# One expert moved out of the last token group, its neighbour's sums rewritten around their swap, and the last drain in 128x64 tiles

## The chip, the cores and the metric

One core of a Trainium2 chip. The metric is the device time of one execution in microseconds (us); the time before is the median of three runs.

## The reference

Two blocks in a row. The first is an attention with a polynomial sketch (batch 4, 4 heads, 1088 positions, head size 32) whose output is laid out as 4352 tokens of 128 features. The second is a mixture of 8 experts over all tokens, weighted by a Sinkhorn-normalised routing. The change is in the second block alone:

```python
def _moe_ref(x, w_gate, w1, w2):
    N, D = x.shape                      # 4352, 128
    E = w_gate.shape[1]                 # 8
    logits = x @ w_gate
    ...                                 # P: 8 Sinkhorn rounds over exp(logits)
    out = np.zeros((N, D), dtype=np.float32)
    for e in range(E):
        h = np.maximum(x @ w1[e], 0.0)  # hidden size 1024
        ye = h @ w2[e]
        out += P[:, e:e + 1] * ye
    return out.astype(np.float32)
```

All of it is in fp32. Inside the profile one fp32 matmul of the program shows as two matmul records and two weight loads.

## The kernel before, in words

The attention, the routing and some experts for the first tokens run first; the change does not touch them. The function `weighted()` does the rest, in the token groups of the list `wgroups`: a group is a start, a width `n` and a list of experts, and holds 2n tokens in two halves. Five groups of 2 x 256 tokens go through experts 1 to 7, three of 2 x 224 through experts 2 to 7, one of 2 x 224 (tokens 3904 to 4351) through experts 2, 1, 3, 4, 5, and the last group takes the same tokens through the experts left. The order of experts is turned round in every other group, so that neighbours share a loaded expert. Each group adds its result to what `kept` holds for its tokens.

Both layers are cut into 2 x 2 blocks. A product of blocks in 64x64 tiles is one unit of TensorE's work: four matmuls (two row halves, two column halves), eight records. The first layer takes seven products instead of eight for each half of an expert, by sums of inputs, of weights and of results. So does the second layer, except in groups listed in `whole` (the last group), which take eight products and need fewer sums: four sums of hidden activations on VectorE (L1099 to L1104) fall away there.

The work is a list of steps `todo`: one for each group's expert and each half `s` of it. In the loop at the end of `weighted()` the generators `firsts(t)` (first layer of step t) and `seconds(t - 1)` (second layer of the step before) take turns, product by product. So a step interleaves 7 products of the first layer (L1043, into the PSUM tiles `pair`) with 7 or 8 of the second (L1193, into the PSUM tiles `s`, called `acc`). In `firsts` ScalarE copies three results out (L1122 to L1132), VectorE adds three pairs of them (L1053), ScalarE applies the ReLU (L1056). The next step's first product writes over the `pair` tile that the third add reads. The last `seconds` runs alone, since no first layer is left.

`acc[g][rho][u]` are four PSUM banks of a group: `rho` is the row half that a 64-row matmul used, `u` the token half (in the seven-product form, q). The two banks of one `u` have to be added in the end.

At the end of a group of seven products `ended()` copies two banks out with ScalarE (tile `z`), `add_half()` adds the other two with VectorE (L1242), and `finish_seven()` swaps the upper and lower 64 partitions of `z` into `w` by two DMAs on SP (L1260). The sums after that are put into the list `leisure`. An entry is taken from it by `leave()` at fixed places of later steps, some by GpSimd, most by VectorE; an entry `None` only lets one such place pass. `put()` turns a token half with VectorE (`yt`, L1278), and `store()` writes it out with 4 or 8 DMAs (L681), four for each batch row that it touches. `finish_last()` is the end of the last group: it does what is left in `leisure`, adds both banks to `kept`, turns and stores.

The order is the program's own on each engine and each DMA queue (`tc.manual_schedule()`), so whatever waits holds back what stands behind it. SP issues the DMAs of loads, swaps and stores in one line; only the stores of the last group are shared with ScalarE's queue.

Of the kernel before, what the change touches and what calls it, by code (L numbers as in the profile page):

```python
# [10 lines left out]
F32 = mybir.dt.float32  # L11
# [39 lines left out]
def kernel(  # L51
# [477 lines left out]
    def routing():  # L529
# [45 lines left out]
        for b in (1, 0, 2, 3):  # L575
# [99 lines left out]
    def store(yt, b0, b1, queues=(nc.sync,)):  # L675
        first, k = b0, 0
        while b0 < b1:
            b, a = divmod(b0, SA)
            m = min(b1 - b0, SA - a)
            for r in range(4):  # L680
                queues[k % len(queues)].dma_start(  # L681
                    out=AP(tensor=out.tensor, offset=out[b * S + a, 32 * r].offset,
                           ap=[[SA * DM, 32], [DM, m], [1, 32]]),
                    in_=yt[32 * r:32 * (r + 1), b0 - first:b0 - first + m, :])
                k += 1
            b0 += m
# [323 lines left out]
    def weighted():  # L1010
# [8 lines left out]
        def flat(t, n):  # L1019
            return t.rearrange("p (r n) -> p r n", r=2)  # L1020
# [6 lines left out]
        def firsts(t):  # L1027
# [137 lines left out]
        def seconds(t):  # L1165

            i, s = todo[t]
            g, e = witems[i]
            lo, n, es = wgroups[g]
            h, ts = rooms(t)  # L1170
            coming = next_of(i, 2) if s else None

            def fetch(part_):
                if coming is not None:
                    load_second(coming, part_)

            if g not in acc:
                acc[g] = [[mps.tile([P, 512], F32, tag=f"s{2 * rho + q}", name="s") for q in range(2)]
                          for rho in range(2)]

            def raw(dh, k, r):
                m = ((RAW00, RAW01), (F0, RAW11))[dh][k]
                return form_of(i, m)[:, H2 * (2 * r + s):H2 * (2 * r + s + 1)]

            def form(m, r):
                return form_of(i, (F0, F1, F2, F3)[m])[:, H2 * (2 * r + s):H2 * (2 * r + s + 1)]

            def into(half, w, x, r, q, place):
                per = 2 * len(es) * (3 if q and g != LAST else 4)
                for rho in range(2):  # L1190
                    rows = slice(H2 * rho, H2 * (rho + 1))
                    c = counts[g, rho, q, half] = counts.get((g, rho, q, half), 0) + 1
                    yield lambda rho=rho, rows=rows, c=c: nc.tensor.matmul(  # L1193
                        acc[g][rho][q][H2 * half:H2 * (half + 1), n * place:n * (place + 1)], w[rows],
                        flat(x, n)[rows, r], start=c == 1, stop=c == per, tile_position=(H2 * rho, H2 * half))

            def both(x, y):
                for one, two_ in zip(x, y):
                    one()
                    two_()  # L1200

            last = t + 1 == len(todo) or witems[todo[t + 1][0]][0] != g
            if g in whole:
                for m, (k, u, b) in enumerate(((0, 0, 0), (1, 0, 2), (0, 1, 3), (1, 1, 1))):
                    for r in range(2):
                        both(into(0, raw(0, k, r), h[:, b], r, u, u), into(1, raw(1, k, r), h[:, b], r, u, u))
                        if last and m % 2 and r == 1:
                            finish_last(g, u)
# [22 lines left out]
        ends = {}  # L1231

        def ended(g, q):
            n = wgroups[g][1]
# [4 lines left out]
        def add_half(g, q):  # L1239
            n = wgroups[g][1]  # L1240
            z = ends[g][:, q, 0:2 * n]
            nc.vector.tensor_tensor(z, acc[g][1][q][:, 0:2 * n], z, op=Alu.add)  # L1242

        def settle(g):
            while chores and chores[0][0] <= g:
# [6 lines left out]
        def finish_seven(g):  # L1252
# [5 lines left out]
            t = late[0].tile([P, 3, NW], F32, tag="t", name="t", bufs=1)  # L1258
            for s in range(2):
                nc.sync.dma_start(out=w[H2 * (1 - s):H2 * (2 - s), :, 0:2 * n], in_=z[H2 * s:H2 * (s + 1), :, 0:2 * n])  # L1260
            leisure.extend([None] * (5 if g + 1 == LAST else 3))
# [11 lines left out]
            plus(y[up, 0], t1[up], t3[up])  # L1273
            out_of(g, y)

        def put(y, at, n, queues=(nc.sync,)):
            yt = late[0].tile([P, NW // 32, 32], F32, tag="yt", name="yt", bufs=2)[:, 0:n // 32, :]
            nc.vector.transpose(out=yt.rearrange("p b d -> p (b d)"), in_=y)  # L1278
            store(yt, at // 32, (at + n) // 32, queues)

        def out_of(g, y):
            lo, n, es = wgroups[g]
            for t in range(2):
                at = lo + n * (1 - t)
                k = kept[0][:, at:at + n]
                plus(k if g + 1 == LAST else y[:, t], y[:, t], k)
                if g + 1 < LAST:
                    leisure.append((lambda engine, t=t, at=at: put(y[:, t], at, n), False))

        def finish_last(g, u):  # L1290
            lo, n, es = wgroups[g]
            while leisure:
                do = leisure.pop(0)
                if do:
                    do[0](nc.vector)
            at = lo + n * (1 - u)
            y = kept[0][:, at:at + n]
            for rho in range(2):
                nc.vector.tensor_tensor(y, acc[g][rho][u][:, n * u:n * (u + 1)], y, op=Alu.add)
            put(y, at, n, (nc.sync, nc.scalar))  # L1300

        for t in range(len(todo) + 1):
            if t < len(todo):
# [145 lines left out]
```

## Time and profile before

| | |
|---|---|
| median of 3 runs | 894.93 us (894.17 to 895.25) |
| profiled execution | 893.78 us |
| its span | 892.0 us |
| PE, share of the span | 884.2 us, 99% |
| DVE | 758.1 us, 85% |
| ACT | 546.3 us, 61% |
| POOL | 271.0 us, 30% |
| granted TensorE clock | 1.0 |

PE is TensorE, PEld its weight loads, DVE VectorE, ACT ScalarE, POOL GpSimd, SP the queue of DMA issues. Rows of a timeline give start and duration in us, engine, line, operation, written and read tiles, shapes, count, and in brackets the idle time before with what ended it. The chain of waits is the work that ended last, followed back. Line numbers are those of the kernel before.

### The profile page before, as it was taken

To read this page: it belongs to the slowest core of one execution; us is meant where nothing else is said; L and a number is where in the kernel's file an instruction comes from. 1 tells how busy PE (TensorE), PEld (TensorE's weight loads), DVE (VectorE), ACT (ScalarE), POOL (GpSimd) and SP (SyncE) were. 2 spreads that over 40 slices of the span, in tenths; PEclk is the share of its full clock that TensorE was granted. 3 is DMA by queue.
4 is the path that set the end of the run, shared out by engine and by line. 5 is a ranking of instruction groups with operands and counts; after the bars stand their busy time and mean duration, and the time that the engine had idled before them with its cause. 6 is when DMAs were issued, how large, how long until landed. Compare 5 with 4: busy or idle time off the path is not lost.

```text
span 892.0 us, 36526 instructions
## 1 busy us (share of the span) xinstructions
PE 884.2 (99%) x15372; PEld 630.1 (71%) x15372; DVE 758.1 (85%) x1324; ACT 546.3 (61%) x1087; POOL 271.0 (30%) x307
## 2 busy tenths in 40 slices
PE   9999999999999999999999999999999999999997
PEld 5777644557666777777777777777877887887876
DVE  7578789887998888888888888888898899889885
ACT  3446366645666666666666666666666666666664
POOL 3121126364552223223213312322333222323220
PEclk9999999999999999999999999999999999999999
DMA  9998499686785876487567666665775875885752
GB/s 247 294 282 251 104 237 252 107 231 184 237 259 166 238 218 194 125 233 211 171 170 206 204 174 194 206 174 160 231 221 142 255 212 152 232 256 147 230 172 44
DMA packets 146628, 178.83 MB, mean 200 GB/s; under 512 B 56448, under 2 KB 93904, under 8 KB 146080
## 3 DMA queue, kind: packets, MB, share of 16 engines
q1 hardware_dynamic: 138832, 166.40, 64.5%
q0 software_dynamic: 6528, 9.95, 5.6%
q8 instruction: 122, 2.00, 0.9%
q14 instruction: 42, 0.34, 0.1%
q10 hardware_dynamic: 1104, 0.15, 0.1%
HBM read 133.83 MB, written 25.99 MB: 179 GB/s over the span
## 4 chain that ended last, share of the span: by engine, by line
PE 96%; DVE 2%; ACT 1%; issue 0%; POOL 0%; DVEq 0%; ACTq 0%; POOLq 0%
PE pair L1043 39%; PE s L1193 39%; PE a L711 7%; PE s L772 7%; PE a L305 1%; DVE hb L726 1%; PE a L420 1%; PE a L118 1%; PE a L272 0%; PE s L334 0%; PE a L384 0%; PE s L350 0%; DVE cs L560 0%; PE a L454 0%; PE a L350 0%
## 5 line engine op out<-in xcount | busy, mean ns | idle before, releaser
L1043 PE MATMUL pair<-xf,w1x 64*64 64x256 f32 (+1 forms) x6736 | 496.4, 365 | 0.1
L1043 PEld LDWEIGHTS pair<-xf,w1x 64*64 64x64 f32 x6736 | 255.4, 133 | 93.7 <-DVE hb L1053 6.1
L1053 DVE TENSOR_TENSOR hb<-pair,copies 128x512 f32<-128x512 f32 (+1 forms) x354 | 233.7, 662 | 69.3 <-PE pair L1043 29.9
L1193 PE MATMUL s<-hb,w 64*64 64x256 f32 (+1 forms) x3904 | 290.0, 364 | 0.0
L1193 PE MATMUL s<-hb,ws 64*64 64x256 f32 (+1 forms) x2848 | 213.6, 365 | 0.0
L1056 ACT ACTIVATE hb<-hb 128x512 f32<-128x512 f32 (+1 forms) x240 | 145.6, 608 | 102.0 <-DVE hb L1053 96.7
L1193 PEld LDWEIGHTS s<-hb,w 64*64 64x64 f32 x3904 | 151.9, 133 | 50.2
L973 POOL TENSOR_TENSOR xf<-xT,pb 128x512 f32<-128x512 f32 (+1 forms) x60 | 73.7, 1228 | 263.2 <-ACT xf L1066 216.2
L981 POOL TENSOR_TENSOR xf<-xf 128x512 f32<-128x512 f32 (+1 forms) x59 | 72.5, 1229 | 217.4 <-ACT xf L1066 133.3
L1193 PEld LDWEIGHTS s<-hb,ws 64*64 64x64 f32 x2848 | 111.4, 133 | 36.0
L711 PE MATMUL a<-xT,w 128*64 128x416 f32 (+3 forms) x512 | 121.1, 466 | 0.0
L713 ACT ACTIVATE hb<-a 128x416 f32<-128x416 f32 (+3 forms) x128 | 59.7, 468 | 66.1 <-PE a L711 53.5
L1056 ACT ACTIVATE hb<-pair 128x512 f32<-128x512 f32 (+1 forms) x126 | 72.5, 575 | 43.5 <-PE pair L1043 43.5
L1099 DVE SCALAR_TENSOR_TENSOR hb<-hb 128x512 f32<-128x512 f32 (+1 forms) x116 | 77.9, 671 | 16.5 <-ACT hb L1056 4.6
L1132 ACT COPY copies<-pair 128x512 f32<-128x512 f32 (+1 forms) x118 | 66.5, 564 | 30.6 <-PE pair L1043 30.6
L1129 ACT COPY copies<-pair 128x512 f32<-128x512 f32 (+1 forms) x118 | 66.5, 564 | 29.7 <-PE pair L1043 29.7
L1122 ACT COPY copies<-pair 128x512 f32<-128x512 f32 (+1 forms) x118 | 66.6, 565 | 26.4 <-PE pair L1043 26.4
L1102 DVE TENSOR_TENSOR hb<-hb 128x512 f32<-128x512 f32 (+1 forms) x116 | 77.8, 670 | 3.1 <-ACT z L1237 0.5
L1104 DVE TENSOR_TENSOR hb<-hb 128x512 f32<-128x512 f32 (+1 forms) x116 | 78.9, 680 | 0.0
L1103 DVE SCALAR_TENSOR_TENSOR hb<-hb 128x512 f32<-128x512 f32 (+1 forms) x116 | 78.8, 679 | 0.0
L726 DVE TENSOR_TENSOR hb<-hb 128x416 f32<-128x416 f32 (+7 forms) x84 | 60.5, 720 | 18.4 <-ACT hb L713 12.9
L772 PE MATMUL s<-hb,ws 128*64 128x416 f32 (+3 forms) x224 | 70.9, 475 | 0.6 <-DVE hb L726 0.4
(177 smaller groups left out, 668.2 us busy)
## 6 DMA issues: line engine op xcount, KB each, us to landing
w1x<-w1x SPq DMA_DIRECT2D x135, 256.0 KB, 4.0
w<-w2x SPq DMA_DIRECT2D x102, 256.0 KB, 4.0
ws<-w2x SPq DMA_DIRECT2D x50, 256.0 KB, 3.1
pb<-pT SPq DMA_DIRECT2D x35, 256.0 KB, 4.1
xf<-xf SPq DMA_DIRECT2D x70, 128.0 KB, 2.5
ws<-w2x SPq DMA_DIRECT2D x52, 128.0 KB, 3.6
w1x<-w1x SPq DMA_DIRECT2D x7, 896.0 KB, 5.0
w1x<-w1x SPq DMA_DIRECT2D x45, 128.0 KB, 3.8
```

Source lines behind the costliest of these rows:

```text
L711: nc.tensor.matmul(ph[sl], loaded_w[j][0][:, P * f + H2 * s:P * f + H2 * (s + 1)], xT[:, at + lo:at + hi], start=True, stop=True, tile_pos ...
L772: nc.tensor.matmul(sums[g][i][H2 * s:H2 * (s + 1)], w, x, start=c == 1, stop=c == per, tile_position=(0, H2 * s))
L973: nc.gpsimd.tensor_tensor(xf[:, 0:2].rearrange("p b n -> p (b n)"), xT[:, lo:lo + 2 * n], weights.pop(i), op=Alu.mult)
L981: nc.gpsimd.tensor_tensor(xf[:, 4:6], xf[:, 1:4:2], xf[:, 0:2], op=Alu.subtract)
L1043: nc.tensor.matmul(out[H2 * col:H2 * (col + 1), r], w1[rows, PLACE[form], o:o + H2], xf[rows, x], start=start, stop=stop, tile_position=(H ...
L1053: nc.vector.tensor_tensor(flat(out, n), x, flat(y, n), op=Alu.add)
L1056: nc.scalar.activation(out=x, in_=y, func=Act.Relu)
L1099: nc.vector.scalar_tensor_tensor(ts[:, 0], h[:, 3], 0.0, h[:, 0], op0=Alu.max, op1=Alu.subtract)
L1102: nc.vector.tensor_tensor(ts[:, 2], h[:, 1], ts[:, 0], op=Alu.subtract)
L1103: nc.vector.scalar_tensor_tensor(ts[:, 1], h[:, 3], 0.0, h[:, 1], op0=Alu.max, op1=Alu.subtract)
L1104: nc.vector.tensor_tensor(ts[:, 3], h[:, 2], ts[:, 2], op=Alu.subtract)
L1193: yield lambda rho=rho, rows=rows, c=c: nc.tensor.matmul(acc[g][rho][q][H2 * half:H2 * (half + 1), n * place:n * (place + 1)], w[rows], fl ...
```

## The change

The last group keeps expert 7 alone; expert 6 goes to the group next to it, which runs in the seven-product form. The last step's second layer is done in tiles of 128 rows and 64 columns, which sum both row halves in one bank, in three parts: the first token half, then 128 and 96 columns of the second. `begin_last()` adds the banks of the half step before; `finish_last()` then adds, and turns, each part as it is ready, and stores by token half. The group next to the last gets its own end: each half of its sums is swapped as soon as it is ready, in two DMAs of 64x448 and 64x224, and `finish_next_to_last()` adds most of them directly to `kept`. `firsts` takes three entries of `leisure` ahead of the first half of expert 7 and two ahead of the second half.

In the compiled order the leftovers of the group before (a transpose, a sum, a transpose, and 12 stores on SP) come at the start of the first half of expert 7; the four DMAs of the swap follow the 12 stores on SP's queue. On VectorE the last five sums of `finish_next_to_last()` that wait for the swap stand behind the adds of the second half of expert 7 and ahead of all of `begin_last()` and `finish_last()`.

```diff
-               (3904, 224, [2, 1, 3, 4, 5]), (3904, 224, [E - 1, E - 2])]
+               (3904, 224, [2, 1, 3, 4, 5, 6]), (3904, 224, [7])]
...
-            if g == LAST and s == 1:
-                for _ in range(2):
+            if g == LAST:
+                for _ in range(2 if s else 3):
                     leave(nc.vector, True)
...
-                per = 2 * len(es) * (3 if q and g != LAST else 4)
+                per = (2 * len(es) - (g == LAST)) * (3 if q and g != LAST else 4)
...
+            if g in whole and last:
+                begin_last(g)
+                for u, cols in ((0, (0, n)), (1, (0, 128)), (1, (128, n))):
+                    for k, b in enumerate(((0, 2), (3, 1))[u]):
+                        for r in range(2):
+                            for half in range(2):
+                                nc.tensor.matmul(
+                                    acc[g][0][u][H2 * half:H2 * (half + 1), n * u + cols[0]:n * u + cols[1]],
+                                    raw(half, k, r), flat(h[:, b], n)[:, r, cols[0]:cols[1]],
+                                    start=False, stop=True, tile_position=(0, H2 * half),
+                                    skip_group_check=True)
+                    finish_last(g, u, cols)
+                yield
+                return
...
-                finish_seven(g)
+                (finish_next_to_last if g + 1 == LAST else finish_seven)(g)
...
         def add_half(g, q):
...
+            if g + 1 == LAST:
+                swap_half(g, q)
+
+        def swap_half(g, q):
+            n = wgroups[g][1]
+            if q == 0:
+                swapped.append(late[0].tile([P, 2, 2 * NW], F32, tag="w", name="w", bufs=1).rearrange(
+                    "p q n -> p (q n)")[:, 0:3 * n])
+            w, z = swapped[0], ends[g][:, q]
+            for to, from_, at, lo, hi in (((lower, upper, n, 0, 2 * n), (upper, lower, 2 * n, 0, n)),
+                                          ((lower, upper, 0, 0, n), (upper, lower, 0, 0, 2 * n)))[q]:
+                nc.sync.dma_start(out=w[to, at:at + hi - lo], in_=z[from_, lo:hi])
+
+        def finish_next_to_last(g):
+            settle(g)
+            lo, n, es = wgroups[g]
+            v = [[ends[g][:, q, n * a:n * (a + 1)] for a in range(2)] for q in range(2)]
+            c, a, b = (swapped[0][:, n * m:n * (m + 1)] for m in range(3))
+            k0, k1 = (kept[0][:, lo + n * (1 - u):lo + n * (2 - u)] for u in range(2))
+            t = late[0].tile([P, 3, NW], F32, tag="t", name="t", bufs=1)[:, 0, 0:n]
+            nc.gpsimd.tensor_copy(t[lower], v[0][0][lower])
+            nc.gpsimd.tensor_copy(t[upper], v[1][0][upper])
+            plus(k1[lower], k1[lower], v[0][1][lower], Alu.subtract)
+            plus(k1[upper], k1[upper], v[0][1][upper])
+            plus(k0[lower], k0[lower], v[0][0][lower])
+            plus(k0[upper], k0[upper], v[1][1][upper])
+            plus(t, t, c)
+            plus(k0, k0, a)
+            plus(t, t, b)
+            plus(k0[upper], k0[upper], t[upper])
+            plus(k1, k1, t)
...
+        def begin_last(g):
             while leisure:
                 do = leisure.pop(0)
                 if do:
                     do[0](nc.vector)
+            for u in range(2):
+                at, n = last_of(g, u)
+                y = kept[0][:, at:at + n]
+                nc.vector.tensor_tensor(y, acc[g][1][u][:, n * u:n * (u + 1)], y, op=Alu.add)
+
+        def finish_last(g, u, cols):
+            at, n = last_of(g, u)
+            if cols[0] == 0:
+                ends[g, u] = late[0].tile([P, NW // 32, 32], F32, tag="yt", name="yt", bufs=2)[:, 0:n // 32, :]
+            yt = ends[g, u]
+            y = kept[0][:, at + cols[0]:at + cols[1]]
+            nc.vector.tensor_tensor(y, acc[g][0][u][:, n * u + cols[0]:n * u + cols[1]], y, op=Alu.add)
+            nc.vector.transpose(out=yt[:, cols[0] // 32:cols[1] // 32].rearrange("p b d -> p (b d)"), in_=y)
+            if cols[1] == n:
+                store(yt, at // 32, (at + n) // 32, (nc.sync, nc.scalar))
```

More of the change, by code (lines that the diff above doesn't have):

```diff
@@ L1202, in seconds @@
             last = t + 1 == len(todo) or witems[todo[t + 1][0]][0] != g
+            if g in whole and last:
[12 more added lines that the diff above has]
+                return
             if g in whole:
-                for m, (k, u, b) in enumerate(((0, 0, 0), (1, 0, 2), (0, 1, 3), (1, 1, 1))):
+                for k, u, b in ((0, 0, 0), (1, 0, 2), (0, 1, 3), (1, 1, 1)):
                     for r in range(2):
                         both(into(0, raw(0, k, r), h[:, b], r, u, u), into(1, raw(1, k, r), h[:, b], r, u, u))
-                        if last and m % 2 and r == 1:
-                            finish_last(g, u)
                         yield
@@ L1226, in seconds @@
                 add_half(g, 1)
-                finish_seven(g)
+                (finish_next_to_last if g + 1 == LAST else finish_seven)(g)
                 ending.clear()
             yield
-        ends = {}
+        ends, swapped = {}, []
         def ended(g, q):
@@ L1260, in finish_seven @@
                 nc.sync.dma_start(out=w[H2 * (1 - s):H2 * (2 - s), :, 0:2 * n], in_=z[H2 * s:H2 * (s + 1), :, 0:2 * n])
[L1261 removed]
+            leisure.extend([None] * 3)
             v, x = ([[u[:, q, n * a:n * (a + 1)] for a in range(2)] for q in range(2)] for u in (z, w))
@@ L1284, in out_of, with last_of @@
                 at = lo + n * (1 - t)
[L1285 to L1290, printed above, removed]
+                plus(y[:, t], y[:, t], kept[0][:, at:at + n])
+                leisure.append((lambda engine, t=t, at=at: put(y[:, t], at, n), False))
+        def last_of(g, u):
             lo, n, es = wgroups[g]
+            return lo + n * (1 - u), n
+        def begin_last(g):
             while leisure:
@@ L1295, in finish_last @@
                     do[0](nc.vector)
[L1296 to L1300, printed above, removed]
+            for u in range(2):
[12 more added lines that the diff above has]
+                store(yt, at // 32, (at + n) // 32, (nc.sync, nc.scalar))
         for t in range(len(todo) + 1):
```

4 lines of the change are left out of this document (2 added, 2 removed).

## The prediction

> **What bounds the kernel now.** I read the page first, for the engine shares and the chain, then the windows of the last steps, then the timelines of TensorE (PE), VectorE (DVE) and of SP's queue in the last 30 us.
>
> ```profile
> span 892.0 us, 36526 instructions
> PE 96%; DVE 2%; ACT 1%; issue 0%; POOL 0%; DVEq 0%; ACTq 0%; POOLq 0%
> ```
>
> The chain is TensorE for 96% of the span. The change touches nothing ahead of the last item but one, so only the last steps count. Windows of the last steps (time, then busy us by engine, granted clock, DMA share):
>
> ```profile
> 858.90:864.20 5.30, 5.30 (x120) 4.28 (x116) 4.91 (x9) 3.30 (x6) 2.43 (x3) 1.00 0.61 193
> 869.50:875.20 5.70, 5.70 (x127) 4.58 (x120) 3.44 (x9) 4.03 (x9) 1.86 (x2) 1.00 0.44 101
> ```
>
> The first is a step of the group next to the last: 14 products in 5.30 us, with VectorE at 4.91. The second is a step of the last group: 15 products. From the chain in order of time, PE's last stretch and the work behind it:
>
> ```profile
> 883.52 3.79 PE s L1193 x80
> 887.31 0.02 issue
> 887.33 0.40 DVE kept L1299
> ...
> 887.83 0.40 DVE kept L1299
> 888.23 0.03 issue
> 888.26 0.41 DVE yt L1278
> ```
>
> 80 records are ten products of eight: 0.379 us each. After PE's end come 1.36 us of VectorE up to 888.67, then the last stores: 3.33 us to the end of the span. The profiled execution took 893.78, 1.78 over its span and 1.15 under the median of 894.93; I work in the span's clock and add the difference to the median.
>
> **PE's products.** An expert of the last group costs 2 x 8 products of the second layer, in the group next to it 2 x 7. Moving expert 6 removes two: -0.76 us. The last drain in 128x64 tiles streams the same work:
>
> ```profile
> 149.59 0.51 PE L772 MATMUL s<-hb,ws 128*64 128x416 f32 x1
> ...
> 149.93 0.51 PE L772 MATMUL s<-hb,ws 128*64 128x416 f32 x1
> ...
> 150.28 0.51 PE L772 MATMUL s<-hb,ws 128*64 128x416 f32 x1
> ```
>
> Here two 128x64 tiles (the other, of L711, runs beside it) take 0.345 us per 416 columns, 0.83 ns a column. Four 64x64 tiles of 224 columns take half of 0.379, 0.85 ns a column. So the eight products stay at 3.03 us. The Trainium skill, "TensorE: Matmul & The Clock Gate", Part 3 (The mechanism), says that a weight load overlaps running matmuls only where its row group differs; tiles of 128 rows have no other row group. The row just shown speaks against a charge here; the rule's result is a rival below.
>
> **VectorE ahead of the new last item.** Expert 6 in the seven-product form needs four more VectorE sums a step, as its neighbours do; 5.30 us steps hold them. But three leftover operations of an earlier group (transpose, add, transpose) now stand ahead of the first add of item 7, first half.
>
> ```profile
> 848.32 2.07 DVE L1053 TENSOR_TENSOR hb<-pair,copies 128x448 f32<-128x448 f32 x3 [0.30 <-ACT xf L1066]
> ...
> 852.94 0.38 DVE L985 TENSOR_TENSOR xf<-xf 128x224 f32<-128x224 f32 x1
> ```
> ```profile
> 864.21 1.31 DVE L1053 TENSOR_TENSOR hb<-pair,copies 128x448 f32<-128x448 f32 x2
> 865.44 0.61 DVE L1242 TENSOR_TENSOR z<-s,z 128x448 f32<-128x448 f32 x1
> 865.97 0.61 DVE L1053 TENSOR_TENSOR hb<-pair,copies 128x448 f32<-128x448 f32 x1
> ...
> 872.02 0.38 DVE L983 TENSOR_TENSOR xf<-xf 128x224 f32<-128x224 f32 x1
> 872.32 0.40 DVE L1278 STREAM_TRANSPOSE yt<-y 128x224 f32<-128x224 f32 x1
> 872.65 0.35 DVE L1250 TENSOR_TENSOR y<-y,kept 128x224 f32<-128x224 f32 x1
> 872.92 0.38 DVE L985 TENSOR_TENSOR xf<-xf 128x224 f32<-128x224 f32 x1
> ```
>
> A step's last sum starts 4.62 after its first add (848.32 to 852.94). In the new order the two half steps of expert 6 begin at 864.21 and 869.51, so that sum starts at 874.13 and the first transpose 0.30 later, 874.43. Transpose, add, transpose start 0.33, 0.27 and 0.33 apart, so the first add of item 7 starts at 875.36 instead of 864.21 + 10.60 = 874.81: 0.55 late. From there VectorE runs without a gap to the third add (865.97 + 0.61, 2.37 after the first), on which PE's next step waits:
>
> ```profile
> 866.16 0.56 PE L1193 MATMUL s<-hb,ws 64*64 64x224 f32 x8
> 866.64 0.61 PE L1043 MATMUL pair<-xf,w1x 64*64 64x224 f32 x8
> ```
>
> 866.64 stands 0.06 behind the end of that add, and 0.10 behind PE's own pace: there is no slack, and the 0.55 passes to PE. PE: -0.76 + 0.55 = -0.21, end near 887.10; item 7's second half starts at 866.64 + 10.60 + 0.55 = 877.79.
>
> **SP's queue ahead of the swap.** Each leftover transpose issues its stores on SP, 12 in all, and the four swap DMAs come behind them in SP's order. The same 12 in the trace of before, and the issue of two DMAs of the swap's larger shape:
>
> ```profile
> 872.75 6.35 SPq L681 DMA_DIRECT2D out_dram<-yt  x12
> ```
> ```profile
> 854.89 1.11 SPq L976 DMA_DIRECT2D xf<-xf  x2
> ```
>
> The first store goes 0.43 after the first transpose starts (872.32, 872.75): 874.86. SP is through at 881.21. The sums whose swap comes last are ready earlier:
>
> ```profile
> 868.08 0.62 DVE L1242 TENSOR_TENSOR z<-s,z 128x448 f32<-128x448 f32 x1 [1.50 <-ACT z L1237]
> ```
>
> This add ends 2.06 after 866.64, so at 879.85 in the new order. The swap is thus not held by its data but by the stores: the first pair goes at 881.21, the second at 882.32, its last DMA at 882.88. Landing after issue, smallest, median and largest, of the rows that swap halves for the inputs (L976, the same shape) and of the old swap (L1260, twice the bytes):
>
> ```profile
> DMA to landing us min/median/max: 2.1/3.0/6.7
> ```
> ```profile
> DMA to landing us min/median/max: 3.0/3.2/4.0
> ```
>
> I take 2.8, a little under 3.0 because the weights are all in by then; bounds 2.1 and 4.0. It lands at 885.7. The Trainium skill, "DMA: Bandwidth & Descriptors", Anatomy of one DMA, gives about 2.0 us plus bytes over 436 GB/s for a DMA of the GpSimd path; my estimate from that page for 0.11 MB is 2.3, and the sum would be 0.5 lower by it. Most of this case's landings are longer.
>
> **The sums after the swap.** In the new order the first operation that needs the late swap stands directly behind item 7's adds, so VectorE waits from about 883.6 to 885.75. Nothing of PE's is queued behind that wait; the whole final drain is.
>
> ```profile
> 883.48 0.39 DVE L1250 TENSOR_TENSOR t<-t,w 64x224 f32<-64x224 f32 x1
> ...
> 885.95 0.88 DVE L1299 TENSOR_TENSOR kept<-s,kept 128x224 f32<-128x224 f32 x2
> 886.86 0.41 DVE L1278 STREAM_TRANSPOSE yt<-kept 128x224 f32<-128x224 f32 x1
> 887.33 0.89 DVE L1299 TENSOR_TENSOR kept<-s,kept 128x224 f32<-128x224 f32 x2
> ```
>
> Seven SBUF sums took 885.95 - 883.48 = 2.47, 0.35 each; five remain behind the swap: 1.75. Then come two adds of the other bank, the first half's add and transpose, and two adds and transposes of 128 and 96 columns. Before, four adds and two transposes took 888.67 - 885.95 = 2.72. One split part more but the same columns in all, and fewer neighbours that depend on each other: I keep 2.7 (2.3 to 3.1). End: 885.75 + 1.75 + 2.7 = 890.2 against 888.67, **+1.5 us**. PE, done at 887.1, is hidden behind VectorE, and so is its saving, and the saving of splitting the last half.
>
> GpSimd's two new copies and one sum of 64x224 lie within the wait for the swap. Expert 6's full set of forms adds 0.38 MB of loads (256 KB instead of 128, and 256 KB more) near 863, where the window shows DMA 0.61 busy: nothing.
>
> The sum: 893.78 + 1.5 = 895.3 for the profiled execution, 894.93 + 1.5 = **896.4** for the median.
>
> **Rivals.**
> - *The stores drain in time.* If SP passes the 12 stores sooner, the last swap DMA goes when its data allows, 0.06 and one issue of 0.56 after 879.85: at 880.5, and lands by 883.3. Then 1.75 + 2.7 lead to 887.8, while PE's end asks for 887.10 + 0.65 (adding and turning 96 columns, about half of a full half's 0.40 and 0.41 with their gaps) = 887.75: both near 887.8, 0.9 better, 894.0. For: the long store in the row of 12 may not recur. Against: 6.35 is measured, and the order is fixed. Chance 0.15.
> - *The swap stalls at issue.* The old swap's issue reaches 1.84 us beside a median of 0.60:
>
> ```profile
> L1260 SPq DMA_DIRECT2D w<-z x18: 461/596/1836, 287.0 to 869.4; - x18
> ```
>
>   One such stall adds 1.24 at the head of the same chain: 897.7, slower than before by 2.7. It decides, against the bound of 0.2% (1.8 us, about what a measurement tells from no change), once the stall or a longer landing exceeds 0.3 us beyond my sum. Chance 0.22.
> - *Weight loads of 128x64 tiles don't hide.* 24 pairs of passes (8 each of 224, 128 and 96 columns) would each show a load of 0.133:
>
> ```profile
> 868.77 0.13 PEld L1193 LDWEIGHTS s<-hb,w 64*64 64x64 f32 x1
> ```
>
>   PE's end 887.10 + 3.2 = 890.3, plus 0.65 for the last quarter: 890.95, so +2.3, 897.2. This is what the rule of the Trainium skill named above would bring. The 0.345 us spacing speaks against it. Chance 0.03.
> - *All savings in full*: no delay at item 7, no wait for the swap: -0.76 - (1.36 - 0.65) = -1.5, 893.5. Chance 0.05.
>
> **How the numbers follow.** The forecast has 0.55 and its own range 895.5 to 897.3 (landing 2.1 to 3.2, sums +-0.4). The range over the cases, 893.9 to 897.8, takes in the early swap and the stall. Slower by over 0.2% means above 896.7: the stall, the weight rival and the upper third of the forecast, with the runs' spread of 1.1: 0.37. Faster by over 0.2% means below 893.1, under every case here: 0.05. Within: 0.58.
>
> **What the profile after would show.** Right: 12 stores on SP from about 874.9 to 881.2, swap DMAs directly behind; VectorE idle some 2 us ahead of a sum of t and w, ended by a DMA; PE's end near 887.1 and VectorE's last transpose near 890.2. Wrong: swap DMAs at their data's time (877 and 880), a last transpose within 0.8 us of PE's end, or gaps between the 128x64 pairs.

## Result, and the profile after

Slower. In alternation on one chip the changed kernel took a median of 898.41 us (897.35 to 900.42, 8 runs), the kernel before 895.29 (894.17 to 897.18, 8 runs): a ratio of 1.0037, interval 1.0027 to 1.0047. I had forecast 1.5 us more, no change that a measurement can tell, and a range up to 897.8. It came to about twice that, and most of the second half by a mechanism that none of the rivals named.

The profiled execution took 898.37 us, 4.59 more than that of before. Part of this lies at the very start, where nothing was changed. One VectorE group of the first stage, in the trace of before and then of after (start, duration, engine, line, operation, and in brackets the idle time before it):

```profile
8.88 2.69 DVE L289 TENSOR_TENSOR kp<-ab 128x1024 f32<-128x1024 f32 x3 [0.86 <-ACT ab L275]
```
```profile
10.36 2.69 DVE L289 TENSOR_TENSOR kp<-ab 128x1024 f32<-128x1024 f32 x3 [2.59 <-ACT ab L275]
```

Over the twelve traces of this study this group starts anywhere from 8.83 to 10.36, so two traces can't be compared by their spans. From here on I count from the first add of expert 6's first half, the last point that all the kernels share. It lies anywhere from 863.69 to 867.37 in these traces, at 864.21 in before, and in after:

```profile
865.63 0.62 DVE L1053 TENSOR_TENSOR hb<-pair,copies 128x448 f32<-128x448 f32 x1
```

So 1.42 is to be taken off a time of after to set it beside one of before or of the prediction. What is left, 3.17 of the 4.59, arises behind that add, and agrees with the medians' 3.12.

The page of after, whole span and share of the chain by engine:

```profile
span 896.6 us, 36479 instructions
...
PE 94%; DVE 4%; ACT 1%; issue 0%; DMA 0%; SPq 0%; POOL 0%; DVEq 0%; POOLq 0%
```

VectorE's share has gone from 2% to 4%, but little of that belongs to the change. VectorE's part of the chain behind 860 us has grown from 2.9 to 5.9 us; between 120 and 250 us, where nothing was changed, it has grown from 18.7 to 29.2. New in the chain are the steps of a DMA and of SP's queue. The timeline of SP's queue in after:

```profile
876.28 6.82 SPq L681 DMA_DIRECT2D out_dram<-yt  x12
883.21 2.38 SPq L1268 DMA_DIRECT2D w<-z  x4
```

The chain of waits, its step from the last of these four DMAs, and then PE's last stretch:

```profile
885.00 2.30 DMA w<-z
...
890.80 1.49 PE s L1209 x16
```

And VectorE's timeline:

```profile
875.85 0.41 DVE L1324 STREAM_TRANSPOSE yt<-y 128x224 f32<-128x224 f32 x1
...
876.90 1.12 DVE L1053 TENSOR_TENSOR hb<-pair,copies 128x448 f32<-128x448 f32 x2
...
880.58 0.62 DVE L1254 TENSOR_TENSOR z<-s,z 128x448 f32<-128x448 f32 x1 [1.50 <-ACT z L1249]
...
887.38 0.39 DVE L1296 TENSOR_TENSOR t<-t,w 128x224 f32<-128x224 f32 x1 [2.35 <-DMA w<-z]
...
889.14 0.68 DVE L1346 TENSOR_TENSOR kept<-s,kept 128x224 f32<-128x224 f32 x2
...
890.49 0.25 DVE L1354 TENSOR_TENSOR kept<-s,kept 128x128 f32<-128x128 f32 x1
890.78 0.31 DVE L1355 STREAM_TRANSPOSE yt<-kept 128x128 f32<-128x128 f32 x1
892.31 0.26 DVE L1354 TENSOR_TENSOR kept<-s,kept 128x96 f32<-128x96 f32 x1 [1.22 <-PE s L1209]
892.60 0.28 DVE L1355 STREAM_TRANSPOSE yt<-kept 128x96 f32<-128x96 f32 x1
```

Down to 889.14 this is the chain of the prediction: stores, then the swap behind them, then a wait for the DMA, then five sums. The last two rows are not: VectorE waits 1.22 us for PE, which should have been done long before. PE's timeline says why, from the last matmul of the 128 columns on:

```profile
887.70 0.27 PE L1209 MATMUL s<-hb,ws 128*64 128x128 f32 x1
890.80 0.98 PE L1209 MATMUL s<-hb,w 128*64 128x96 f32 x9 [2.83 <-DVE kept L1354]
...
891.57 0.36 PE L1209 MATMUL s<-hb,w 128*64 128x96 f32 x1
...
891.73 0.36 PE L1209 MATMUL s<-hb,w 128*64 128x96 f32 x1
```

PE stands idle for 2.83 us between the two column ranges and starts 0.06 after VectorE's add over the first 128 columns (890.49 + 0.25). In the view of waits it is PE's longest of the whole execution:

```profile
PE s L1209 <- DVE kept L1354: 2.8, 1, 2.8
```

The add reads columns 224 to 351 of a PSUM tile, the matmuls behind it write columns 352 to 447 of the same tile, in one bank. No column is shared. Still the first of these matmuls waits for that add. And then they run slowly. Windows of the drain (time, then busy us by engine, granted clock, DMA share, GB/s):

```profile
884.00:887.90 3.90, 3.90 (x64) 2.85 (x56) 1.52 (x4) 1.53 (x3) 0.00 (x0) 1.00 0.38 88
887.90:890.79 2.89, 0.07 (x2) 0.00 (x0) 2.75 (x10) 0.00 (x0) 0.00 (x0) 1.00 0.00 0
890.79:892.30 1.51, 1.47 (x16) 1.18 (x16) 0.30 (x1) 0.00 (x0) 0.00 (x0) 0.54 0.50 78
```

Behind the gap the granted clock is 0.54 in the mean. Pairs of 96 columns start 0.16 apart (891.57, 891.73); in the second experiment, where PE does not pause, they start 0.09 apart or less.

The last transpose ends at 892.88, in before's clock 891.46 against 888.67: 2.79 later. Of this 1.5 was forecast. The other 1.26 (891.46 against the 890.2 forecast) splits at the end of the five sums: 0.22 lies ahead of it (889.14 less 1.42 is 887.72, forecast 887.50), and 1.04 behind it, where PE's wait is. From the last transpose to the end of the span are 3.70 us instead of 3.33, another 0.37; over all the traces these last stores take between 3.27 and 3.70. The sum of the three, 1.5 + 1.26 + 0.37, is 3.13 of the 3.17.

### The profile page after: what moved, and what is told of

Same layout as the page of the kernel before. It is cut to its first block, busy times and chain, and to the rows that moved or that the text cites. A ratio compares the mean times of both kernels' runs of the same rounds, so it can differ in the third digit from the quotient of the medians.

```text
span 896.6 us, 36479 instructions
## 1 busy us (share of the span) xinstructions
PE 885.9 (99%) x15340; PEld 629.6 (70%) x15340; DVE 763.5 (85%) x1332; ACT 545.8 (61%) x1085; POOL 272.0 (30%) x309
## 3 DMA queue, kind: packets, MB, share of 16 engines
HBM read 134.22 MB, written 25.99 MB: 179 GB/s over the span
## 4 chain that ended last, share of the span: by engine, by line
PE 94%; DVE 4%; ACT 1%; issue 0%; DMA 0%; SPq 0%; POOL 0%; DVEq 0%; POOLq 0%
PE pair L1043 38%; PE s L1193 37%; PE a L711 7%; PE s L772 6%; DVE hb L726 1%; PE a L305 1%; PE a L118 1%; PE a L420 1%; PE a L272 0%; DVE hb L1053 0%; PE s L334 0%; PE a L384 0%; DMA w<-z 0%; PE s L350 0%; PE a L454 0%
## 5 line engine op out<-in xcount | busy, mean ns | idle before, releaser
L1193 PE MATMUL s<-hb,w 64*64 64x256 f32 (+1 forms) x3824 | 282.9, 365 | 0.0
L1193 PE MATMUL s<-hb,ws 64*64 64x256 f32 (+1 forms) x2848 | 211.0, 365 | 0.0
L1193 PEld LDWEIGHTS s<-hb,w 64*64 64x64 f32 x3824 | 147.1, 133 | 49.1
L1099 DVE SCALAR_TENSOR_TENSOR hb<-hb 128x512 f32<-128x512 f32 (+1 forms) x118 | 79.2, 671 | 16.7 <-ACT hb L1056 4.6
L1102 DVE TENSOR_TENSOR hb<-hb 128x512 f32<-128x512 f32 (+1 forms) x118 | 79.2, 671 | 3.1 <-ACT z L1249 0.5
L1104 DVE TENSOR_TENSOR hb<-hb 128x512 f32<-128x512 f32 (+1 forms) x118 | 80.3, 680 | 0.0
L1103 DVE SCALAR_TENSOR_TENSOR hb<-hb 128x512 f32<-128x512 f32 (+1 forms) x118 | 80.2, 679 | 0.0
```

Source lines behind the costliest of these rows:

```text
L1099: nc.vector.scalar_tensor_tensor(ts[:, 0], h[:, 3], 0.0, h[:, 0], op0=Alu.max, op1=Alu.subtract)
L1102: nc.vector.tensor_tensor(ts[:, 2], h[:, 1], ts[:, 0], op=Alu.subtract)
L1103: nc.vector.scalar_tensor_tensor(ts[:, 1], h[:, 3], 0.0, h[:, 1], op0=Alu.max, op1=Alu.subtract)
L1104: nc.vector.tensor_tensor(ts[:, 3], h[:, 2], ts[:, 2], op=Alu.subtract)
L1193: yield lambda rho=rho, rows=rows, c=c: nc.tensor.matmul(acc[g][rho][q][H2 * half:H2 * (half + 1), n * place:n * (place + 1)], w[rows], fl ...
```

## Experiments

My theory after that reading: (a) the swap behind the twelve stores delays VectorE's end by some 3 us against its data, as forecast; (b) beside it, the split puts PE behind VectorE through the shared bank. The rival to (b): VectorE's chain alone makes the end, and PE's gap only fills time that VectorE needs anyway. The rival to (a): landing and sums, not the queue, make the end late. The times of all, where the columns "last transpose" and "span" count from the first add of expert 6's first half in the one profiled execution, and the ratio is to the kernel before, run in alternation:

| kernel | that add at | last transpose ends | span ends | median us | before, same session | ratio (95%) |
|---|---|---|---|---|---|---|
| before | 864.21 | 24.46 | 27.78 | | | 1 |
| the change | 865.63 | 27.25 | 30.95 | 898.41 | 895.29 | 1.0037 (1.0027 to 1.0047) |
| unsplit | 863.69 | 25.18 | 28.85 | 896.35 | 895.38 | 1.0013 (1.0004 to 1.0022) |
| two_leaves | 866.40 | 24.20 | 27.57 | 895.02 | 895.38 | 0.9998 (0.9990 to 1.0007) |
| other_bank | 865.94 | 25.85 | 29.36 | 896.79 | 895.38 | 1.0013 (1.0004 to 1.0023) |
| other_bank_two | 864.33 | 23.88 | 27.32 | 894.23 | 895.38 | 0.9990 (0.9979 to 1.0002) |
| both | 867.37 | 23.43 | 26.86 | 894.94 | 895.72 | 0.9989 (0.9979 to 0.9999) |
| drain_whole | 865.34 | 24.13 | 27.52 | 895.46 | 895.47 | 1.0001 (0.9990 to 1.0011) |
| drain_split | 865.45 | 24.90 | 28.24 | 895.94 | 895.47 | 1.0008 (0.9995 to 1.0021) |
| old_sums | 866.38 | 29.59 | 32.86 | 900.89 | 895.47 | 1.0056 (1.0039 to 1.0074) |
| early_sums | 863.98 | 24.51 | 27.88 | 894.89 | 895.47 | 0.9992 (0.9981 to 1.0002) |
| third_room | 865.56 | 23.55 | 27.03 | 894.41 | 895.72 | 0.9983 (0.9972 to 0.9994) |

The change was not run again beside the later kernels. The median of before lies between 895.29 and 895.72 in the four sessions, so a difference of medians from two sessions holds to some 0.4 us.

### unsplit: the last half in one column range

```diff
-                for u, cols in ((0, (0, n)), (1, (0, 128)), (1, (128, n))):
+                for u, cols in ((0, (0, n)), (1, (0, n))):
```

> The last token half in one piece of 224 columns instead of 128 and 96; all else as changed. Theory (the last quarter's matmuls wait for VectorE's add over the first 128 columns of the same PSUM bank, 2.8 us of idle TensorE and then eight pairs at 0.16 instead of 0.08 us): no gap of TensorE in the last drain beyond 0.5 us, the granted clock stays at 1.0 until TensorE is done, and the last transpose ends 1.5 us earlier after the sums that wait for the swap; time 1.5 us under the changed kernel. Rival (VectorE's late sums set the end alone, the wait lies beside them): last transpose within 0.4 us of the changed kernel's, time the same. Rival (the 128x64 tiles are slow by themselves): the drain takes clearly over 3.03 us here too.

The end of VectorE's timeline:

```profile
887.74 0.41 DVE L1355 STREAM_TRANSPOSE yt<-kept 128x224 f32<-128x224 f32 x1
888.08 0.35 DVE L1354 TENSOR_TENSOR kept<-s,kept 128x224 f32<-128x224 f32 x1
888.46 0.41 DVE L1355 STREAM_TRANSPOSE yt<-kept 128x224 f32<-128x224 f32 x1
```

No row of it waits for PE, and PE waits for no read of the drain. The last transpose ends 2.07 earlier than in the change, the median is 2.06 lower. Not all of that is the split's: the twelve stores took SP 6.34 here instead of 6.82, and the first swapped sum comes 0.47 sooner behind the common add. From that sum on the tail is 1.60 shorter, with 1.5 expected. The rival to (b) falls: PE's gap was on the path. The rival of slow 128x64 tiles falls too: PE's drain runs from 883.65 to 886.66, at clock 1.00. The split made the tail longer by about 1.6 us where it stood.

### other_bank: the split kept, its two parts in two other banks

```diff
+                def sink(u, cols):
+                    if u:
+                        return pairs[cols[0] > 0][:, 1, 0:cols[1] - cols[0]]
+                    return acc[g][0][u][:, n * u + cols[0]:n * u + cols[1]]
...
-                                    start=False, stop=True, tile_position=(0, H2 * half),
+                                    start=u == 1 and k == r == 0, stop=True, tile_position=(0, H2 * half),
...
+            nc.vector.tensor_tensor(y, acc[g][0][1][:, n:2 * n], y, op=Alu.add)
```

The two ranges are summed into two free banks of `pairs`; what the old bank holds costs VectorE one add more.

> The last half's two parts (128 and 96 columns) are summed in two PSUM banks of their own, and one more VectorE add of 224 columns brings in what the old bank held; three leftovers, all else as changed. Theory (the wait is one for the bank, not for the columns): TensorE goes through the whole drain without a gap, at clock 1.0; the last transpose ends 1.0 us earlier (the wait and the slow clock gone, one add more); time 1.0 us under the changed kernel. Rival (the matmuls of 96 columns are slow by their shape): their eight pairs stay at 0.16 us each without the gap.

PE's timeline, the last column range, and VectorE's two last rows:

```profile
888.10 0.58 PE L1216 MATMUL pair<-hb,w 128*64 128x96 f32 x9
...
888.51 0.25 PE L1216 MATMUL pair<-hb,w 128*64 128x96 f32 x1
...
888.60 0.25 PE L1216 MATMUL pair<-hb,w 128*64 128x96 f32 x1
```
```profile
891.25 0.22 DVE L1363 TENSOR_TENSOR kept<-pair,kept 128x96 f32<-128x96 f32 x1
891.50 0.28 DVE L1364 STREAM_TRANSPOSE yt<-kept 128x96 f32<-128x96 f32 x1
```

But for the one add, the same instructions in the same order and shapes: no wait, pairs 0.09 us apart or less instead of 0.16, the last transpose 1.40 earlier, the median 1.62 lower. As in unsplit a part, 0.49, comes from quicker stores (6.32 instead of 6.82). From the first swapped sum on the tail is 0.92 shorter in spite of one add more. So it is the shared place of the two ranges, not the split or the 96 columns, that held PE.

Two things stay open. The wait is one that the compiled program has, for a semaphore of VectorE; what the chip would do without it no run shows. And here a bank is also one tile of the program (`acc` is made of tiles of one bank each, and the two new places lie in two tiles), so these runs can't tell a wait for the bank from a wait for the tile.

This kernel is also the change as the prediction had pictured it: its last transpose ends 25.85 behind the add, and the prediction's 890.2 is 25.99 behind 864.21. That they are so close is in part luck: there is one add in it that the forecast did not have (0.31 from its start to that of the next), and the first swapped sum came 0.28 sooner than forecast.

The Trainium skill, "PSUM — Partial Sum Buffer", PSUM bank collisions raise a hardware error, has accesses of two engines kept apart by bank and quadrant of partitions, not by address; a different address in the same bank and quadrant still collides. The wait in the compiled program agrees: 2.83 us in one bank, none in two. "Perfetto Trace Analysis", Matmuls, of the Trainium skill advises turning through the banks, so that the emptying of one goes on beside the matmuls of the next; these two kernels show what that is worth here, the 0.92 us above.

### two_leaves: one leftover piece less ahead of the last item

```diff
-                for _ in range(2 if s else 3):
+                for _ in range(2):
```

The second leftover transpose, and with it eight of the twelve stores, goes behind the swap. The split is kept.

> Two leftovers instead of three ahead of the first half of expert 7, so that 8 of the 12 stores come behind the swap on SP's queue; all else as changed. Theory (the stores hold the swap): the swap's last DMA is issued some 3 us earlier, within 1 us of the sums it carries; the first sum that needs it starts 2.5 us earlier; the last quarter still waits for the add ahead of it, but only some 0.3 us; last transpose 3.4 us earlier, time 3 to 3.5 us under the changed kernel, about the kernel before or 0.3 under it. Rival (the swap's landing or its data are late, not its issue): the first sum that needs it moves by less than 0.5 us, time by less than 0.7.

SP's queue, PE's second column range and a window over it:

```profile
877.05 1.80 SPq L681 DMA_DIRECT2D out_dram<-yt  x4
878.97 4.28 SPq L1268 DMA_DIRECT2D w<-z  x4
883.35 8.09 SPq L681 DMA_DIRECT2D out_dram<-yt  x12
```
```profile
889.11 0.63 PE L1209 MATMUL s<-hb,w 128*64 128x96 f32 x9 [0.80 <-DVE kept L1354]
...
889.57 0.25 PE L1209 MATMUL s<-hb,w 128*64 128x96 f32 x1
...
889.65 0.25 PE L1209 MATMUL s<-hb,w 128*64 128x96 f32 x1
```
```profile
888.00:890.00 2.00, 1.19 (x22) 0.76 (x18) 1.33 (x5) 0.00 (x0) 0.00 (x0) 1.00 0.10 15
```

The swap's last DMA is issued 3.7 us earlier after the common add (15.7 instead of 19.4), and the first swapped sum no longer waits for a DMA. The median is 3.39 lower, back at the kernel before. That is (a): the twelve stores ahead of the swap, not the landing or the sums. A smaller part is not the queue: with one leftover less ahead of it, item 7's first add starts 0.45 sooner behind the common add (10.82 instead of 11.27). The gap of PE is still there, only short: it ends with VectorE's add, and VectorE comes sooner. After 0.80 us idle the granted clock is 1.00 and the pairs are 0.08 apart, so a restart alone does not make the pairs slow.

### other_bank_two and both: the two remedies together

*other_bank_two* has the edits of other_bank and two_leaves, *both* those of unsplit and two_leaves.

> Both edits together: two leftovers ahead of the first half of expert 7 and own banks for the last half's parts. Theory: the two costs are in series only while the swap is late; with the early swap the end is set by TensorE and VectorE nearly together, so time 3 to 3.6 us under the changed kernel, within 0.4 us of the run with two leftovers alone, and 0 to 0.6 us under the kernel before. Rival (the two costs add up independently): 1 us more than the run with two leftovers alone.

> The last half in one piece and two leftovers ahead of the first half of expert 7; all else as changed. Theory (with an early swap the split is worth little either way: it saves VectorE's add and transpose over 128 columns behind TensorE, and costs a standstill of 1.1 us): no gap of TensorE in the drain, last transpose 0.2 to 0.5 us earlier than with two leftovers and the split, time 0 to 0.5 us under that run, 0.4 to 0.8 under the kernel before. Rival (the two repairs add up in full): 2 us under the run with two leftovers alone.

The end of VectorE's timeline in other_bank_two:

```profile
887.68 0.22 DVE L1363 TENSOR_TENSOR kept<-pair,kept 128x96 f32<-128x96 f32 x1
887.93 0.28 DVE L1364 STREAM_TRANSPOSE yt<-kept 128x96 f32<-128x96 f32 x1
```

Each alone took off 1.6 (the bank) and 3.4 (the queue), together 4.2, not 5.0 (3 to 3.6 expected). The gap's length depends on when VectorE gets to its add, so with the swap early there is less left for the other bank to save: 0.32 by the last transpose, 0.79 by the medians. The theory had up to 0.4 and the rival 1, so the medians do not decide between them. The same with the split undone: 0.77 by the last transpose against two_leaves, where I had expected 0.2 to 0.5; the medians of the two come from two sessions and lie 0.42 apart when each session's before is taken off. These steps are near what the timing resolves; that both kernels end a little ahead of before (0.9990 with an interval that holds 1, and 0.9989 with one that just does not) is all I take from them.

### drain_whole and drain_split: the new drain alone

The kernel before with only its last drain in 128x64 tiles, the last half whole or in two column ranges. Experts, sums and swap are as before.

```diff
+            if g in whole and last:
+                begin_last(g)
+                for u, cols in ((0, (0, n)), (1, (0, n))):
...
+                    finish_last(g, u, cols)
```

drain_split has the three parts `((0, (0, n)), (1, (0, 128)), (1, (128, n)))` in that line.

> The kernel before, with only its last drain changed: 128x64 tiles, the second token half in one piece; experts 7 and 6 stay in the last group, sums as before. Theory (the drain in 128x64 tiles streams as fast as in 64x64 tiles and saves one add and its wait behind TensorE): TensorE's end as before, last transpose 0.4 to 0.6 us earlier, time 0.5 us under the kernel before. Rival (weight loads of 128x64 tiles don't hide): the drain some 2 us longer, time 1.5 us over.

> The same, with the second half in 128 and 96 columns of one bank. Theory (the last quarter waits for VectorE's add over the 128 columns): TensorE stands still ahead of the last quarter for 1.0 to 1.3 us although no swap is late, last transpose 0.4 us later than in the kernel before, time 0.3 to 0.6 over it and 0.8 to 1.0 over the run with the half in one piece. Rival (the wait bites only where the sums are late): as fast as the run in one piece or 0.2 faster.

The last transpose of drain_whole, and PE's second column range in drain_split:

```profile
889.05 0.41 DVE L1323 STREAM_TRANSPOSE yt<-kept 128x224 f32<-128x224 f32 x1
```
```profile
888.85 0.63 PE L1209 MATMUL s<-hb,w 128*64 128x96 f32 x9 [0.80 <-DVE kept L1322]
```

The 128x64 tiles gain 0.33 in the trace and nothing that the timing can tell (0.01; 0.5 was expected). The split takes 0.77 back in the trace: with no swap late, PE still waits 0.80, since VectorE comes to that read only behind the first half's add and transpose. By the medians it is 0.48 over drain_whole, and its interval against before holds 1. So in the traces the split in one bank is a loss in both surroundings, smaller where VectorE is early and larger where it is late; the timing of drain_split alone would not show it.

### old_sums: the change with the former sums

The moved expert and the new drain stay; the group next to the last ends as the other groups do, with one swap of both halves and eleven sums behind it.

```diff
-                (finish_next_to_last if g + 1 == LAST else finish_seven)(g)
+                finish_seven(g)
...
-            if g + 1 == LAST:
-                swap_half(g, q)
```

> The changed kernel with the sums of the group next to the last as they were: one swap of all sums at its end and eleven sums behind it; expert 6 moved and the drain in 128x64 tiles with the split half, as changed. Theory (VectorE's chain behind the late swap sets the end, and the rewriting shortens it): the swap is issued at the same time, but about six more sums of 0.35 us stand behind it; last transpose some 2 us later than in the changed kernel, time 2 us over it. Rival (the rewriting itself is the loss): time under the changed kernel.

The first sum behind the swap, the second column range on PE, the window over it:

```profile
888.13 0.38 DVE L1294 TENSOR_TENSOR y<-z,w 64x224 f32<-64x224 f32 x1 [2.78 <-DMA w<-z]
```
```profile
893.80 1.06 PE L1209 MATMUL s<-hb,w 128*64 128x96 f32 x9 [5.09 <-DVE kept L1354]
```
```profile
893.00:895.00 2.00, 1.20 (x16) 1.20 (x16) 1.02 (x4) 0.00 (x0) 0.00 (x0) 0.50 0.21 31
```

2.48 slower than the change by the medians of two sessions, and 2.34 later by the last transpose. The first swapped sum comes at the same place (21.76 behind the common add, 21.75 in the change), so the difference arises behind it. The rewriting of the sums is thus a gain of about 2.3 to 2.5 where it stands; the loss lies in the other edits. PE's gap has grown with VectorE's delay, from 2.83 to 5.09, and the clock behind it is 0.50.

### early_sums and third_room: three sums in a gap of VectorE

The row at 880.58 above has 1.50 us of idle time before it. *early_sums* is other_bank_two with three of the four sums that need no swap put there, and *third_room* the same with three buffers instead of two for the turned halves.

```diff
+            elif g == LAST:
+                early_sums(ending[0])
...
+        def early_sums(g):
...
+            nc.vector.tensor_tensor(k1[lower], k1[lower], v[1][lower], op=Alu.subtract)
+            nc.vector.tensor_tensor(k1[upper], k1[upper], v[1][upper], op=Alu.add)
+            nc.vector.tensor_tensor(k0[lower], k0[lower], v[0][lower], op=Alu.add)
...
-            yt = late[0].tile([P, NW // 32, 32], F32, tag="yt", name="yt", bufs=2)[:, 0:n // 32, :]
+            yt = late[0].tile([P, NW // 32, 32], F32, tag="yt", name="yt", bufs=3)[:, 0:n // 32, :]
```

The three lines go from `finish_next_to_last()` in return. The last two lines, with `yt`, are third_room's alone; it has them in `put()` and in `finish_last()`.

> Own banks for the last half and two leftovers, as in the run with both, and three of the sums that need no swap placed in VectorE's idle time ahead of the last add of the group (so one swapped sum falls to GpSimd). Theory (there VectorE's chain behind the swap still ends 0.65 us behind TensorE's own end): 1.2 us less of VectorE's work behind the adds of expert 7, then TensorE sets the end; last transpose 0.6 to 0.7 us earlier than with both edits, time 0.5 to 0.7 us under it, some 1.7 us under the kernel before. Rival (the swap's landing sets the chain): the sums wait for the swap instead and the end moves by less than 0.3 us.

> The run with the early sums, with three instead of two buffers for the turned halves. Theory (in that run the transpose of the 128 columns stood still 1.1 us for the late stores that still read its buffer): no idle time ahead of that transpose, the last transpose 1.0 us earlier than with two buffers and 0.4 earlier than in the run with both edits; time 1.0 us under the run with early sums, about 1.6 under the kernel before. Rival (another wait: the transpose waits for the add or for TensorE): the idle time stays, time the same.

VectorE's timeline over the 128 columns in early_sums, then in third_room:

```profile
886.36 0.25 DVE L1370 TENSOR_TENSOR kept<-pair,kept 128x128 f32<-128x128 f32 x1
887.73 0.31 DVE L1371 STREAM_TRANSPOSE yt<-kept 128x128 f32<-128x128 f32 x1 [1.12 <-issue]
```
```profile
888.06 0.25 DVE L1370 TENSOR_TENSOR kept<-pair,kept 128x128 f32<-128x128 f32 x1
888.35 0.31 DVE L1371 STREAM_TRANSPOSE yt<-kept 128x128 f32<-128x128 f32 x1
```

early_sums missed, its last transpose 0.63 later than that of other_bank_two instead of 0.6 to 0.7 earlier: the sums moved, but the transpose of the 128 columns then stood 1.12 us, with a releaser that the trace can't name ("issue"). My guess was its output buffer, which the eight late stores still read. A third buffer is the test: the wait is gone and the last transpose 0.96 earlier (1.0 expected). By the medians, each with its session's before taken off, it is 0.73. third_room is ahead of both kernels: 894.41 against 895.72 for before, 0.9983 (0.9972 to 0.9994), and 0.54% under the change if the two ratios are divided.

## Why the prediction was wrong

Point by point, times of after less 1.42.

- *Leftovers ahead of item 7*: the first leftover transpose forecast at 874.43, measured 875.85 - 1.42 = 874.43. Item 7's first add 875.36, measured 875.48. Right.
- *PE*: PE's end was forecast at 887.10. Where it does not wait (other_bank, 1.73 to take off) its last matmul starts at 888.69 and takes 0.25, so 887.21. Right but for the wait.
- *Weight loads of 128x64 tiles hide*: right. Pairs of 96 columns start 0.08 apart (two_leaves), in less than the 0.14 of one load. By the rule of the Trainium skill weighed in the prediction each load would have shown; the trace does not agree with it. The same section lets a load go ahead for the background weight buffer as well, which the prediction did not weigh.
- *SP's queue*: first store 874.86, as forecast. The twelve took 6.82 instead of 6.35, and the last swap DMA went at 883.58 (885.00 in after) instead of 882.88: 0.70 later, 0.47 of it in the stores, the rest in the step to the swap and in its own four issues. The rival of a stalled issue, with a price of 1.24 at the swap, came about by half, and mostly one place earlier in the queue.
- *Landing*: 2.30 from that issue to the end of the wait, forecast 2.8. By luck that made good for most of the 0.70: the first swapped sum came at 885.96, forecast 885.75. The estimate of 2.3 from the Trainium skill, which I had set aside for the longer rows of this case, agrees with the measured value, though the page gives it for the GpSimd path and these are SP's DMAs.
- *Five sums*: 889.14 - 887.38 = 1.76, forecast 1.75.
- *The rest, 2.7, and PE hidden behind VectorE*: wrong. This is the step that failed: "Nothing of PE's is queued behind that wait; the whole final drain is", and from it "PE, done at 887.1, is hidden behind VectorE". PE's last sixteen matmul records were queued behind it, by way of the bank: the 2.7 became 3.74 (887.72 to 891.46). The prediction did not ask what the two column ranges share. The drain's end became a ping-pong: VectorE's add, then PE's restart, then VectorE again. Without the wait the remaining adds and transposes end 25.85 behind the common add (other_bank), the forecast's 25.99.
- *The clock*: about half of the missed price in this execution. Had the pairs run 0.08 apart behind the gap, as in two_leaves, the sixteen records would have taken 0.88 (889.11 to 889.74 and one matmul of 0.25) instead of 1.49 (890.80 to 892.29): 0.61 of the 1.26.

The split, which I had counted at nothing because VectorE would hide its saving, was the part of the loss that I had missed. "Gaps between the 128x64 pairs" stood in the list of what would prove the forecast wrong, for weight loads that show; a gap between the two column ranges stood neither there nor, with its price, in the range.

One time in the rivals was wrong as well: with early stores the sums were to start when the swap lands, at 883.3, but by the prediction's own account VectorE is busy up to 883.6, so that rival's 887.8 for VectorE is 0.3 too early.

## What to carry to other kernels

Where a drain is split so that one engine can empty the first part while another fills the second, give the parts different PSUM banks: in one bank the second part waited here for the reading of the first, and then every delay of the reader became a delay of the writer. Before leftover work is moved ahead of a step, count its DMAs in the queue that the step's own transfer uses: here eight small stores more cost the swap 3.7 us. Late stores hold their buffer too; in early_sums a third one was worth 1 us of the last 24.5.

## What the hardware showed that was not expected

- **A short pause of PE can halve the clock, and not at once.** Behind 2.83 us idle the granted clock was 0.54, behind 5.09 it was 0.50, behind 0.80 still 1.00. In the change it was full through the whole gap and for 0.13 us of PE's work behind it (1.00 from 890.79 to 890.92), and half from then on (0.50 from 890.93 to 892.30).

  By their clock records, in each of the twelve traces the clock falls once, at the end of a stretch at full clock of 884.05 us (the change, other_bank_two) or 887.47 us (the other ten). The two lie 3.42 us apart, which looks like a fixed step of time at which the clock is decided. So what a pause costs hangs on where it lies in these steps, and not on its length alone; the eight timed runs of the change have a mean granted clock of 0.997 in four cases, as in the trace, and 0.998 in four. The Trainium skill, "TensorE: Matmul & The Clock Gate", Part 1, has two clock states, full and half, and a free-running window of about 3.4 us, an idle one of which throttles. The two states and the step agree. The window need not be idle as a whole: of the 3.42 us up to 890.92 PE worked in the first 0.47 and the last 0.12.
- **A store at issue can stall.** The same twelve stores held SP's queue for 6.32 to 6.83 us in before, after, unsplit, other_bank and old_sums. In the trace of after the last two alone took 2.08, where two of twelve would be 1.14:

```profile
881.02 2.08 SPq L681 DMA_DIRECT2D out_dram<-yt  x2
```

- **The start of an execution varies by 1.5 us** (8.83 to 10.36 for the same VectorE group), about as much as the change was forecast to cost. It goes with the clock: the stretch at full clock begins 3.73 us into the earliest of these traces (drain_split) and 6.87 into the latest (the change), and the group starts later by half of that difference. Up to the common add more is added, from causes that stay open: there the traces differ by 3.7. Lining the traces up at a point behind it was needed before any term of 0.5 us could be read.
